# Packed attention and a three-way maximum layer: two of the three lists that order the work, written anew

## The chip, the cores and the metric

The kernel runs on one core of a Trainium2 chip. The metric is the device time of one execution in microseconds (us), as the median of several runs. TensorE is called PE below, VectorE DVE, ScalarE ACT, GpSimd POOL, and SyncE, which here does nothing but issue DMAs, SP.

## The reference

Eight batches, eight heads, 576 positions, 64 features per head, all in float32. First a few packed queries `p` look at keys and values, then the real queries look at what those have packed; the result goes through three matrices, of which the larger value counts, and a fourth.

```python
p_packed = sm_attn(p, k, v)                # softmax(p k^T / 8) v: 32 x 64 per head
out = sm_attn(q, p_packed, p_packed)       # 576 x 64 per head
x = out.transpose(0, 2, 1, 3).reshape(B * S, H * D)          # 4608 x 512
h = np.maximum(np.maximum(x @ w1, x @ w2), x @ w3)           # 4608 x 768
return (h @ w_out).astype(np.float32)                        # 4608 x 512
```

## The kernel before, in words

Everything is worked off batch by batch. For one batch: `scores` (PE, tile `s`) takes packed queries against keys; `weigh` is the exponential (a reduction on DVE, then ACT); `spread` turns the weights by two DVE transposes into `x` and by sixteen DMAs on SP (line 339) from `x` into `xt`; `values` (PE, tile `av`, line 357, 80 small matmuls) multiplies them with v; `packed` turns the result by one PE transpose (line 372), and it is copied into `pt`; `queries` (PE, tile `s2`, shown as `s` of line 386) takes q against `pt`; `attend` is the second softmax, a chain of some ten operations over DVE, POOL and ACT. Then `project` (tile `pw`) multiplies `pt` with the weights, `layer_in` (tiles `m...`) makes the products for the three-way maximum, `maximum` takes it on DVE (tile `r`), `halves` combines and splits `r` into high and low parts (`yah`, `yal`, `ybl`, `ych`, `ycl`, ...), `layer_out` (tiles `mo`) is the last product, and `finish` scales it and stores it (tiles `s`, `t`, `u`, `v` of line 813; the first two batches at line 736, with `r`). Each large float32 product is three matmuls on rounded parts (high by high, low by high, high by low), each 128 x 288.

Nothing but three lists of words sets the order. `START` does batches 0 and 1, converts the weights, and does the attention of batch 2; `LOOP` is run five times, for b = 2 to 6; `LAST` finishes batch 7. A word is a letter for a stage and the indices it is for; each time it stands in a list, the stage goes one step on. In `LOOP` the first digit is added to b, so that a run of it does the layers of batch b and the attention of batch b + 1: `S1` is `scores` of b + 1, `X1` `spread` (its third word issues the sixteen DMAs), `V101` `values`, `K1` `packed`, `Q1` `queries`, `N03` a step of `layer_in`, `H01` of `halves`, `B10` of `attend`. Lower-case words load: `v11` is v of batch b + 1 and its second half of the heads (two DMAs, lines 184 and 185), `q10`, `k20`, `w..` likewise. A letter at the end, `v`, `g` or `a`, puts a movable step onto DVE, POOL or ACT. `J2` has PE multiply the identity to no use (line 162).

Every engine, SP's queue too, works in the order of the list, and waits by semaphores. Of the tiles, k, v, q, `x`, `xt` and `r` share eight buffers, taken in the order of the list, and the products share four single PSUM banks and two double ones; an instruction that needs a buffer waits for the last reader of what lay there.

```python
nc.sync.dma_start(out=v[:, 0:SF, :], in_=va[u].rearrange("p (t x) -> p t x", x=256))
nc.sync.dma_start(out=v[0:SR, SF, :], in_=vb[u])
...
for c in range(4):
    n = len(range(c, NT, 4))
    for i in range(4):
        nc.sync.dma_start(out=at[NP * c:NP * c + NP, 0:n, i], in_=x[NP * i:NP * i + NP, c::4])
...
run(START, 0)
for b in range(2, B - 1):
    run(LOOP, b)
run(LAST, B - 1)
```

Of the kernel before, what the change touches and what calls it, by code (L numbers as in the profile page):

```python
# [52 lines left out]
C12 B011 B001 P00 C12 C12 J21 P01 k10 B000v B000 B010a B001 C20 w32 k11 w21 B000a B000g B010 B001a N00 B010v
B010 B010g C22 C22 P01 P00 B010g N00 B001 B011v B001g v11 J2 S1 v10 B011 P01 C32 C32 N01 N01 N01 C20 B011 w30
E000v C22 B011v B001 E010a A11 A11 A10 A10 E010 Z11 B001v C21 C20 C21 C22 N00 B001v B011 E000 A10 A11 q10 A10v
E000 q11 A11a N00 B011g B011 B011a V101 C20 C30 C30 w31 B011g Z10 E010 N01 V101 C21 C21 K1 C30 N00 w52 C31 K1v
C32 C32 Q1 N00 E011a E001a B10 C31 w41 P02 P02 B11 C52 P10 P10 B10 w40 B11 k20 C40 C41 C31 P02 N01 E011 C30
N01 C31 P03 B10g P03 E001 E001 C41 N02 N02 E020a N02 C52 N02 E011 k21 N02 H00g w42 B10 B11g P10 E021a P03 S2
C40 E020 C40 N03 N03 N03 v21 C41 C41 C42 E020 B11 C42 B10 E021 C52 E030a C42 A20 A20 A21 A21 w50 C50 w51 B11
B11a B10a X2 X2 C50 C50 C51 N02 C52 N03 C40 C42 P04 C51 C50 B10 E030 E030 P11 B11 N03 B11g N03 C51 B10g P04  # L60
C51 P04 E031a N04 N04 N04 P05 E031 B11 v20 B11a E040v E040 B10 H01a H01v N04 N04 N04 E021 w61 E031 H00a H00g
Z20 P05 w60 C60 P05 N05 E041a E041 N05 E041 C61 C61 B10g B10v H01v P11 B11g N10 E050a H02v E040 H04g N10 N10
C60 X2 Z21 H04a H02a V201 P11 N05 C60 H04v E100a C61 C61 E100 C60 E050 E050 w62 C62 N05 N05 E051a E051 N10 N10
w65 C65 E101a W0v W0g W0g R1v N11 w64 q20 V201 K2 K2a C65 C65 N11 N11 E110a E101 N11 w63 H03a H02v E110 E110
C65 H03v E100 W0a q21 C63 Q2 B20 B21 N11 N11 E111v E111 E111 W0g W0a C63 C63 P13 P15 C64 P13 P13 H03v C64 N10
C62 C62 N05 C64 P15 W0g P15 N13 N13 N13 H01v P12 W0g W0a C62 B21 P14 C63 E130a E051 P12 B21g N13 N13 N15 N15
E150a E101 E130 H01a P12 N12 W1g k30 C64 H10v N12 N12 W2g W2g E131v E131 E120a H03v W1g W1v E130 W2v E120 E120
W1a E150 N13 E131 H05a N12 N15 N15 W1v H05v H05g W2a W2v W2a H05g W0g E150 P14 P14 N12 N12 E121a E151a O0 N15
N14 N14 E121 E121 E151 B21 B21 B21v H01g B21 H03a B20 E140a N14 N14 N14 F0 W1a E140 E140 W2v W2v R2g O0 F0 W1v
O0 O0 E141a B21v H05a B20v B20 H03v H12v W1v F0 F0 H05v W2a H10a W1a W1g N14 E141 E141 N15 E151 H13g O0 F0 O0  # L70
O0 O0 O0 O0 O0 H11a H12a H12v H10v W2v k31 F0 R0v O0 O0 F0 F0 F0 H13v H14g H14a H13g H13v F0 O0 H11v H11g R3g
P22 P22 B20 B20v P20 B20 H11v F0 F0 F0 F0 H11a F0 F0 H14v B20v B21 H15a O1 O1 H13a H15v H15g H15v O1 O1 F1 P20
P20 O1 O1 H11v B20 H15a H15v H13v O1 P22 P22 P20 P20g P22g P22g F1 B21a F1 F1 F1 F1 F1 O1 O1 O1 F1 F1 R4g B20a
B20g T2g T2g P21 B21v T2v T2g T2a T2v O1 F1 F1 P20v P20g P21 P21 P21 P21 P21 P21 P21v P22v F1 F1 O1 O1 F1 P20a
P20v P20 T2a O1 P21g P21g P21a T2g R5g P22a P22g F1 P21g F1 P20 P20 P22
# [7 lines left out]
N02 E02 E02 P05 E02 E02 H01g H01g v11 N03 E03v P03a N02 E02 N03 N03 P03g E03a E03a N03 N03 H01g N03 N03 P05
E03 E03a P05v P05g E03 N03 P04 V101 P05v H02v E03 E03 E03 Z11 N03 P05g P04 P04 P04 P04 P04 P04 V101 V101 N04
P04g P04g K1 H02a N04 N04 K1a P04g P04a q10 H02v E04v E04a E03 Q1 P05g B10 B10 P04g N04 E04a H01a E04 N04 N04
N04 E04a E04 N04 N04 N05 E05a E04 H01g N05 N05 N05 E04 E05a E05a H03a A10 N05 N05 N05 E04 E04 B11 B10g B10
H04g H04g E05 P10 P12 B11 E05a P11 N05 H04v B11g P11 P12 P11 P11 P05 P12 E05 E05 N05 E05 B10 B10a O0 O0 O0 O0
E05 E05 F0 P11 B10 P11 P12 P11 P12v H05a H03g H03g H05v P10 H03v B11 F0 F0 H05g F0 B11 B11a B11 O0 O0 O0 H03a
P11g B10v B10 k21 F0 P10 F0 P11v P11g H03v O0 H05g H05a H05v O0 O0 P05 P12g P12g F0 F0 P05 F0 P10 P10g B10a
B10g B11g F0 B11 B11a P12a P10g O0 O0 T1g F0 O0 P10v P10g T1v F0 B11v T1v P11a T1v T1a T1v P10v T1a T1g P10  # L90
P11g F0 P10 O0 P10 F0 P12g P12 P12 P12
"""


# [810 lines left out]
```

## Time and profile before

| | |
|---|---|
| time, median of 3 runs | 463.65 us (462.92 to 464.65) |
| the profiled execution | 462.4 us, its span 460.3 us |
| granted clock of TensorE | 1.00 |
| PE busy | 451.2 us, 98% |
| DVE busy | 392.7 us, 85% |
| POOL busy | 290.3 us, 63% |
| ACT busy | 253.0 us, 55% |
| moved by DMA | 55.68 MB |

The span is from the first to the last instruction of the trace; the execution's own time is 2.1 us more, and the median 1.25 us above that. Matmuls overlap each other, so PE's busy share says that there is nearly always one in flight, not that none came late.

### The profile page before, as it was taken

To read this page: it belongs to the slowest core of one execution; us is meant where nothing else is said; L and a number is where in the kernel's file an instruction comes from. 1 tells how busy PE (TensorE), PEld (TensorE's weight loads), DVE (VectorE), ACT (ScalarE), POOL (GpSimd) and SP (SyncE) were. 2 spreads that over 40 slices of the span, in tenths; PEclk is the share of its full clock that TensorE was granted. 3 is DMA by queue.
4 is the path that set the end of the run, shared out by engine and by line. 5 is a ranking of instruction groups with operands and counts; after the bars stand their busy time and mean duration, and the time that the engine had idled before them with its cause. 6 is when DMAs were issued, how large, how long until landed. Compare 5 with 4: busy or idle time off the path is not lost.

```text
span 460.3 us, 11868 instructions
## 1 busy us (share of the span) xinstructions
PE 451.2 (98%) x4616; PEld 393.2 (85%) x4616; DVE 392.7 (85%) x820; ACT 253.0 (55%) x559; POOL 290.3 (63%) x296
## 2 busy tenths in 40 slices
...
GB/s 316 398 385 339 340 67 269 2 0 115 78 53 141 145 168 1 51 225 104 99 1 85 211 150 34 5 189 122 164 2 53 168 115 30 2 103 1 2 1 103
DMA packets 35783, 55.68 MB, mean 121 GB/s; under 512 B 17296, under 2 KB 26512, under 8 KB 35728
## 3 DMA queue, kind: packets, MB, share of 16 engines
...
q8 instruction: 36, 0.59, 0.5%
q14 instruction: 19, 0.16, 0.1%
...
## 4 chain that ended last, share of the span: by engine, by line
PE 87%; DMA 6%; DVE 5%; issue 1%; ACT 0%; SPq 0%; DVEq 0%
PE mo L784 22%; PE mi L630 12%; PE me L543 9%; PE mx L543 9%; PE pw L459 7%; PE mf L543 6%; PE mu L543 6%; PE mo L707 4%; PE my L543 3%; DMA q<-in_qt 3%; DMA wi<-in_wi 2%; PE av L357 2%; PE s L273 2%; PE s L386 2%; PE idle L162 1%; DMA v<-in_va 1%
## 5 line engine op out<-in xcount | busy, mean ns | idle before, releaser
L486 POOL TENSOR_TENSOR pf<-pf 128x128 f32<-128x128 f32 x73 | 40.8, 569 | 32.0 <-ACT pf L469 23.6
L672 POOL TENSOR_TENSOR r<-r 128x288 f32<-128x288 f32 (+1 forms) x46 | 49.3, 1079 | 14.5 <-DVE r L587 6.6
L477 DVE SCALAR_TENSOR_TENSOR pl<-pw,ph 128x384 fp32r<-128x384 f32 (+1 forms) x67 | 46.6, 719 | 4.1 <-ACT ph L475 3.8
L475 ACT ACTIVATE ph<-pw 128x384 fp32r<-128x384 f32 (+1 forms) x67 | 40.4, 638 | 7.7 <-PE pw L459 7.3
L630 PE MATMUL mi<-a2h,ph 128*128 128x288 f32 x144 | 44.3, 307 | 0.1
L469 ACT ACTIVATE pf<-pw 128x256 f32<-128x256 f32 (+1 forms) x54 | 22.2, 457 | 40.1 <-PE pw L459 40.1
L630 PE MATMUL mi<-a2l,ph 128*128 128x288 f32 x144 | 42.5, 295 | 0.0
L630 PE MATMUL mi<-a2h,pl 128*128 128x288 f32 x144 | 42.4, 295 | 0.0
L459 PE MATMUL pw<-w_sb,pt 64*32 64x384 f32 x768 | 38.3, 489 | 1.2 <-POOL w_sb L225 1.1
L153 POOL TENSOR_TENSOR sl<-pf,sh 128x384 fp32r<-128x384 f32 x30 | 30.5, 1026 | 12.1 <-ACT sh L148 11.8
L225 POOL TENSOR_TENSOR w_sb<-w_sb,wi 128x512 int32<-128x512 int32 x18 | 23.7, 1326 | 22.6 <-DVE w_sb L221 15.7
L630 PEld LDWEIGHTS mi<-a2h,ph 128*128 128x128 f32 x144 | 27.0, 188 | 7.0 <-issue 2.8
L543 PE MATMUL me<-a2h,ph 128*128 128x288 f32 x108 | 32.7, 303 | 0.0
L784 PE MATMUL mo<-ych,xl 128*128 128x288 f32 x108 | 31.9, 295 | 0.0
L543 PE MATMUL me<-a2l,ph 128*128 128x288 f32 x108 | 31.9, 295 | 0.0
L543 PE MATMUL me<-a2h,pl 128*128 128x288 f32 x108 | 31.9, 295 | 0.0
L784 PE MATMUL mo<-ych,xh 128*128 128x288 f32 x108 | 31.8, 295 | 0.0
L784 PE MATMUL mo<-ycl,xh 128*128 128x288 f32 x108 | 31.8, 294 | 0.0
L630 PEld LDWEIGHTS mi<-a2l,ph 128*128 128x128 f32 x144 | 27.0, 188 | 0.1
L630 PEld LDWEIGHTS mi<-a2h,pl 128*128 128x128 f32 x144 | 27.0, 188 | 0.0
L148 ACT COPY r<-me 128x288 f32<-128x288 f32 x25 | 10.0, 400 | 30.9 <-PE me L543 30.4
L543 PEld LDWEIGHTS me<-a2h,ph 128*128 128x128 f32 x108 | 20.3, 188 | 5.4 <-DVE r L587 3.1
...
## 6 DMA issues: line engine op xcount, KB each, us to landing
...
q<-in_qt SPq DMA_DIRECT2D x16, 576.0 KB, 5.0
...
```

The costliest lines, as they stand in the source:

```text
L153: on(default).tensor_tensor(out=lo, in0=src, in1=hi.bitcast(F32), op=ALU.subtract)
L225: nc.gpsimd.tensor_tensor(out=dst.bitcast(I32), in0=dst.bitcast(I32), in1=up, op=ALU.add)
L459: nc.tensor.matmul(out=ps[r][NP * n:NP * n + NP, 0:NW * P], lhsT=pt_sb[b % 2][o, NP * n:NP * n + NP], rhs=w_sb[o, j, n * NW * P:(n + 1) * ...
L469: nc.scalar.activation(out=f[:, r], in_=x[:, :, 0:2 * P], func=AF.Copy, scale=2.0 ** -WS)
L475: nc.scalar.activation(out=hi[:, r], in_=x, func=AF.Copy, scale=2.0 ** -WS)
L477: nc.vector.scalar_tensor_tensor(out=lo[:, r], in0=x, scalar=2.0 ** -WS, in1=hi[:, r].bitcast(F32), op0=ALU.mult, op1=ALU.subtract,)
L486: on("g").tensor_tensor(out=f[:, k], in0=f[:, x], in1=f[:, y], op=op)
L543: nc.tensor.matmul(out=ps[:, 0:HS], lhsT=w[wi], rhs=x[xi], start=first and n == 0, stop=n == 2, skip_group_check=not first,)
L630: nc.tensor.matmul(out=sums[b, j, hf, x][:, 0:HS], lhsT=w[:, r, x * P:(x + 1) * P], rhs=a[:, c], start=(r == 0 and n == 0), stop=(r == R - ...
L672: less = lambda out, x, y: on("g").tensor_tensor(out=out, in0=x, in1=y, op=ALU.subtract)
L707: nc.tensor.matmul(out=ps[:, 0:HS], lhsT=w[:, x, m * P:(m + 1) * P], rhs=h[:, z], start=(p == 0 and i == 0), stop=(p == NQ - 1 and i == 2),)
L784: nc.tensor.matmul(out=ps[:, 0:HS], lhsT=w[:, x, m * P:(m + 1) * P], rhs=h[:, z], start=(not onto and p == 0 and i == 0), stop=(p == NQ - ...
```

## The change

The text of `LOOP` is written anew, and that of `START` from the word `C12` of its fourth line on. `LAST` and all code are as before. The same steps are done; what differs is their order on each engine, and for some the engine. One dummy matmul, of the word `J2` ahead of batch 1's `scores`, is gone. The core of the diff is the head of `LOOP`:

```diff
-S1 A11 q11 k20 A10 N00 N00 N00 E00a v10 E00a E00v A10 N00 E00 N00 N00 X1 E00a E00 N00 E00 N00 N00 A11 P03 P05
-P03 P03 X1 E00 E00 N01 E00 P03 P03 P03 P03 P03g P03v H00g H00v N01 N01 N01 H00g E01a E01a E01v N01 E01 N01 X1
...
+v11 S1 N00 E00a N00 E00a A10 A10 N00 N00 A11 E00v N00 N00 E00 N00 E00a X1 A11 E00 N00 N00 E00 A11 P03 P03 P05
+N01 N01 N01 N01 X1 E00 E00 E00 P03 v10 P03 P03 q11 P03 k21 P03 E01a E01a N01 E01v E01 N01 N01 E01a N01 N01 E01
...
```

On SP's queue, one run of `LOOP` (b = 3) before. `v8` and `v9` are the two tiles of v of batch 4, `q8` and `q9` of q, `kt10` a tile of k of batch 5, and the sixteen DMAs of `xt4` stand as eight and eight:

```order
L193 DMA q9_2930<-in_qt 128x1152
L178 DMA kt10_2932<-in_kp 128x1280
L184 DMA v8_2955<-in_va 128x1024
L185 DMA v8_2955<-in_vb 64x256
L339 DMA xt4_3064<-x4_2974 32x5x64 x8
L339 DMA xt4_3064<-x4_2974 32x4x64 x8
L184 DMA v9_3157<-in_va 128x1024
L185 DMA v9_3157<-in_vb 64x256
L193 DMA q8_3318<-in_qt 128x1152
L178 DMA kt11_3597<-in_kp 128x1280
```

The same run now:

```order
L184 DMA v9_2906<-in_va 128x1024
L185 DMA v9_2906<-in_vb 64x256
L184 DMA v8_3035<-in_va 128x1024
L185 DMA v8_3035<-in_vb 64x256
L193 DMA q9_3042<-in_qt 128x1152
L178 DMA kt11_3045<-in_kp 128x1280
L339 DMA xt4_3198<-x4_2973 32x5x64 x8
L339 DMA xt4_3198<-x4_2973 32x4x64 x8
L193 DMA q8_3287<-in_qt 128x1152
L178 DMA kt10_3370<-in_kp 128x1280
```

Both tiles of v, one of q and one of k now stand ahead of the sixteen DMAs; before, the second tile of v stood behind them. The second tile of q is behind them in both.

On PE in the same run, from the transpose of `packed` to the first half of `s2` of batch 4, before; `me`, `mx` and `mu` are products of `layer_in` of batch 3:

```order
L372 MATMUL av4_3224<-ident_67,pp4_3291 128x128
L543 MATMUL mx3_4_3306<-a2h3_0_2826,ph3_4_3285 128x288
L543 MATMUL mx3_4_3306<-a2h3_0_2826,pl3_4_3286 128x288
L543 MATMUL mx3_4_3306<-a2l3_0_2828,ph3_4_3285 128x288
L543 MATMUL mu3_4_3310<-th3_0_2881,ph3_4_3285 128x288
L543 MATMUL mu3_4_3310<-th3_0_2881,pl3_4_3286 128x288
L543 MATMUL mu3_4_3310<-tl3_0_2883,ph3_4_3285 128x288
L386 MATMUL s2_4_0_3326<-q8_3318,pt0_73 32x288 x4
L386 MATMUL s2_4_0_3326<-q9_2930,pt0_73 32x288 x4
```

And now:

```order
L372 MATMUL av4_3229<-ident_67,pp4_3293 128x128
L543 MATMUL me3_4_3299<-a2h3_0_2828,ph3_4_3277 128x288
L543 MATMUL me3_4_3299<-a2h3_0_2828,pl3_4_3278 128x288
L543 MATMUL me3_4_3299<-a2l3_0_2830,ph3_4_3277 128x288
L543 MATMUL me3_4_3299<-a2h3_1_2841,ph3_4_3277 128x288
L543 MATMUL me3_4_3299<-a2h3_1_2841,pl3_4_3278 128x288
L543 MATMUL me3_4_3299<-a2l3_1_2843,ph3_4_3277 128x288
L386 MATMUL s2_4_0_3317<-q8_3287,pt0_73 32x288 x4
L386 MATMUL s2_4_0_3317<-q9_3042,pt0_73 32x288 x4
```

Before, twelve matmuls stood between `av` and the transpose and six between the transpose and `s2`; now it is six and six, so `s2` follows `av` six matmuls sooner.

On SP's queue in `START`, behind the sixteen DMAs for batch 2, before; `wi6_2` to `wi6_5` are pieces of the output weights, `q4` and `q5` are q of batch 2:

```order
L339 DMA xt2_1031<-x2_820 32x4x64 x8
L172 DMA wi6_2_1116<-in_wo 128x512
L172 DMA wi6_5_1149<-in_wo 128x512
L172 DMA wi6_4_1168<-in_wo 128x512
L193 DMA q4_1170<-in_qt 128x1152
L172 DMA wi6_3_1203<-in_wo 128x512
L193 DMA q5_1216<-in_qt 128x1152
```

And now:

```order
L339 DMA xt2_1001<-x2_831 32x4x64 x8
L172 DMA wi6_3_1166<-in_wo 128x512
L172 DMA wi6_2_1168<-in_wo 128x512
L193 DMA q5_1200<-in_qt 128x1152
L193 DMA q4_1206<-in_qt 128x1152
L172 DMA wi6_4_1333<-in_wo 128x512
```

Of the output weights' pieces, four stood between the sixteen and the second tile of q; now it is two, one (`wi6_5`) has gone ahead of the sixteen, and one follows q. On PE, 54 matmuls and the transpose stood between `av` of batch 2 and its `s2`; now it is 42 and the transpose.

Between the engines, one run of `LOOP` moves two steps from DVE to POOL, one `ycl` (128x864, line 153) and one product of `attend` (128x576, line 429), and two small ones of line 486; a split of 128x576 (line 153) and a subtraction of 128x288 (line 672) go from POOL to DVE, and the rounding copy `ych` (128x864) and the small `z` of line 425 from ACT to DVE. ACT takes one copy of 128x288 from DVE. In the changed part of `START`, DVE gives up fourteen instructions: one `ycl`, one split each of 128x576, 128x512, 128x384 and 128x288 (line 153), two combinations of 128x256 (line 237), a wide and a narrow subtraction (lines 672 and 415), one small `z`, and four copies out of PSUM. It gets seven: a copy of 128x256, a subtraction of 128x576 (line 415), two small ones of line 486, and one each of lines 505, 514 and 672. Most of what it gives up goes to POOL, whose instructions there rise from 88 to 93.

## Rows read from the trace of the kernel before

**Rows 1.** The page: busy us by engine; loads of q, median us to landing.

```profile
PE 451.2 (98%) x4616; PEld 393.2 (85%) x4616; DVE 392.7 (85%) x820; ACT 253.0 (55%) x559; POOL 290.3 (63%) x296
...
q<-in_qt SPq DMA_DIRECT2D x16, 576.0 KB, 5.0
```

**Rows 2.** Windows: length, busy us (instructions) by engine, granted clock, DMA share, GB/s.

```profile
90.00:127.00 37.00, 36.73 (x295) 35.21 (x294) 35.38 (x62) 17.79 (x34) 22.31 (x20) 1.00 0.20 64
...
233.00:286.00 53.00, 52.50 (x565) 47.09 (x563) 46.74 (x100) 29.45 (x69) 35.48 (x38) 1.00 0.34 104
```

**Rows 3.** Timeline of PE (start us, us): `av` of batches 2, 3, 5.

```profile
68.41 1.46 PE L357 MATMUL av<-v,xt 128*32 128x64 f32 x80
69.80 0.40 PE L630 MATMUL mi<-a2h,ph 128*128 128x288 f32 x1
...
165.02 1.94 PE L357 MATMUL av<-v,xt 128*32 128x64 f32 x80
166.88 0.40 PE L543 MATMUL mf<-a2h,ph 128*128 128x288 f32 x1
...
271.54 0.31 PE L357 MATMUL av<-v,xt 128*32 128x64 f32 x4
272.31 1.54 PE L357 MATMUL av<-v,xt 128*32 128x64 f32 x76 [0.47 <-DMA v<-in_va]
273.78 0.40 PE L543 MATMUL mf<-a2h,ph 128*128 128x288 f32 x1
```

**Rows 4.** Timeline of SP's queue (start us, us of issuing): batch 5 is fetched.

```profile
257.12 11.48 SPq L339 DMA_DIRECT2D xt<-x  x16
268.70 0.53 SPq L184 DMA_DIRECT2D v<-in_va  x1
270.37 0.33 SPq L193 DMA_DIRECT2D q<-in_qt  x1
```

**Rows 5.** DMA traffic of 250 to 275 us in 40 slices of 0.625 us.

```profile
GB/s 354 65 0 0 100 335 155 273 398 368 410 416 410 399 256 89 17 11 63 64 66 66 66 53 53 53 53 53 53 53 34 84 262 408 254 117 292 361 166 57
```

**Rows 6.** Timeline of PE: `s2` of batch 5; two products six matmuls apart.

```profile
276.47 1.20 PE L386 MATMUL s<-q,pt 64*32 64x288 f32 x32
...
278.50 0.29 PE L543 MATMUL me<-a2h,ph 128*128 128x288 f32 x1
279.30 0.31 PE L543 MATMUL mx<-th,sh 128*128 128x288 f32 x1
```

**Rows 7.** Timeline of SP's queue: the rest of batch 2's loads.

```profile
66.89 1.48 SPq L172 DMA_DIRECT2D wi<-in_wo  x3
...
70.98 1.20 SPq L193 DMA_DIRECT2D q<-in_qt  x1
```

**Rows 8.** Timeline of PE: `s2` of batch 2, from q's second tile on.

```profile
79.41 0.72 PE L386 MATMUL s<-q,pt 64*32 64x288 f32 x16 [0.99 <-DMA q<-in_qt]
```

**Rows 9.** Timeline of PE: two waits for DVE, then the dummy.

```profile
126.25 0.40 PE L707 MATMUL mo<-yal,xh 128*128 128x288 f32 x1 [0.27 <-DVE yal L153]
...
133.88 0.40 PE L707 MATMUL mo<-ycl,xh 128*128 128x288 f32 x1 [0.60 <-DVE ycl L153]
...
29.27 0.59 PE L162 MATMUL idle<-ident 128*128 128x256 f32 x2
29.80 0.47 PE L273 MATMUL s<-kt 64*32 64x288 f32 x8
```

**Rows 10.** Timelines of DVE and POOL around 122 us.

```profile
118.87 0.76 DVE L672 TENSOR_TENSOR r<-r 128x576 f32<-128x576 f32 x1
...
122.20 1.87 DVE L672 TENSOR_TENSOR r<-r 128x576 f32<-128x576 f32 x1
...
122.03 1.43 POOL L755 TENSOR_TENSOR t<-v,t 128x576 f32<-128x576 f32 x1
```

**Rows 11.** Groups by form: xcount | busy us, mean ns | idle before, releaser.

```profile
L153 DVE TENSOR_TENSOR ycl<-r,ych 128x864 fp32r<-128x864 f32 x18 | 20.2, 1153 | 0.8 <-POOL ych L150 0.8
...
L153 POOL TENSOR_TENSOR ycl<-r,ych 128x864 fp32r<-128x864 f32 x6 | 12.4, 2060 | 2.2 <-ACT ych L148 2.2
```

More of the change, by code (lines that the diff above doesn't have):

```diff
@@ L52 @@
 B000 B001 B000 B001v B000v C10 C10 C11 C11 C11 B000 C11 B000 B010 w20 C12 J11 P00 P00 w22 B011 P00 B000a B000
[L53 to L75, printed above, removed]
+C12 B011 B001 P00 C12 C12 J21 P01 k10 B000v B000 B010a B001 C20 w32 k11 w21 B000a B000g B010 B001a w30 v11
@@ new lines @@
+B010v C20 v10 B001 B010 B010g B010g B011g P00 N00 B001g P01 P01 C32 C32 B011 N00 C20 S1 C20 C22 B011 B001 A10
+B001g N00 B011v C22 q10 B011 B011g N01 N01 A11 E000a A10 A10 N01 B011 q11 C22 E010a E010 E010 A11 A11 E000
+E000 B001g A10a B011a C32 A11a N00 C21 C30 C30 Z11 w31 C22 C21 B011g Z10 V101 V101 N01 w52 K1 E011a C32 K1a
+N00 E001a C31 C31 Q1 C21 C21 C30 C30 B10 C52 w41 B11 w40 C31 C31 N00 E001 P02 B11 P02 P10 P10 P02 C41 C41 N01
+E011 N01 k20 B11g w42 E001 H00g C52 B10 B10g P03 P03 N02 B11 N02 N02 N02 E020a P10 P03 C42 C40 B10 C41 E021a
@@ new lines @@
+C52 C52 E020 E020 k21 C41 B11 E011 B11a B10 N02 C40 C40 N03 C42 C42 S2 N03 N03 N03 C40 A20 N02 C42 A21 E021
+E030a w51 C51 w50 A20 v21 X2 A21 w60 P04 C50 C50 X2 C50 P11 C51 C50 C51 P04 H00a B10a E030 E030 B11 P04 N03
+E031a E031 N03 C60 C60 B10 B11g B11 B11a E021 N04 E040a v20 B10v C51 E031 B10 N04 E040 P05 N04 N04 P05 B11v
+N04 N04 P05 w65 E041a E041 E041 w61 H00g N05 N05 N05 H03a H03g C61 X2 Z20 E040 B10a H01a N05 E051a B10v N10
+E050v E050 H02g H02a E050 H01v H01g C60 N10 N10 H04v C65 C65 C61 C61 H01v V201 E100a C61 C60 Z21 W0g V201 N10
@@ new lines @@
+N10 P11 P11 E100 N11 K2 H02v E101a N11 w63 w62 E100 K2v W0g N05 H03v C63 E110a E110 N11 W0g N11 q21 H03g W0a
+W0g R1v q20 Q2 W0a C65 C65 C62 E051 N11 H03a N11 E101 P13 C63 C63 B21 P15 B20 E111v E111 E111 E110 H04a W0g
+N05 P13 P13 E051 W0g H01a C63 P15 N10 P15 N13 N13 N13 H04v w64 C64 C64 E130a E130 C62 C62 C64 N13 E131v W0a
+E130 P12 H05a P14 C62 B21 N13 N13 P12 P12 H05g N15 E150a E131 E131 B21v N12 N12 P14 N12 W1g N15 W1g C64 E101
+H10v N12 E120a E120 E120 B21 W1g P14 E150 W2g W2v W1a N14 E140a W2v H05v H05g W0g W1v W1g N15 E150 N15 E151a
@@ new lines @@
+B21 B21a R3v W1g B21 N12 N14 E140 E121a E121 W2a W2v N12 W2a E121 N14 E140 N14 N14 N14 E141a E141 E141 B20 N15
+N15 O0 F0 O0 B20v W2v W2v H14v B20 R2v E151 E151 W1g H12g O0 O0 O0 F0 F0 H01v W2g W2v H05a H10a H03g H05v O0
+F0 H10v H13a F0 F0 H11a H11v H11g O0 H13v W1v F0 W1g O0 F0 R0g H12a H12v O0 F0 H13g O0 O0 O0 B21v B21 k30 H14g
+H11v H11a H15a O0 O0 F0 F0 P20 H13v F0 F0 B20 P22 P22 P22 H14v O1 O1 O1 B20v B20 F0 F0 H15v B20g H13a F0 H15v
+H15v H11v H13v F1 F1 F1 B20 H15a H15g O1 O1 O1 O1 O1 P20 O1 k31 P20 P20 P20v P22 B20a B20g F1 F1 B21a B21v F1
@@ L76 @@
+F1 P21 O1 O1 O1 P21 F1 P22g P21 T2g T2v T2g P20v P20g F1 T2v P22g T2a F1 T2v P21 P21 P21 P21 P21v P22v F1 P21g
+P21v T2a F1 T2g P20a P20g P20 P22a O1 O1 F1 F1 R5g F1 R4g P22g P21a F1 P20 P21g P22 P20
 """
 LOOP = """
-S1 A11 q11 k20 A10 N00 N00 N00 E00a v10 E00a E00v A10 N00 E00 N00 N00 X1 E00a E00 N00 E00 N00 N00 A11 P03 P05
-P03 P03 X1 E00 E00 N01 E00 P03 P03 P03 P03 P03g P03v H00g H00v N01 N01 N01 H00g E01a E01a E01v N01 E01 N01 X1
-E01a N01 N01 N01 E01 N02 N02 N02 E01 P05 E01 E01 E01 E02a E02a A11 Z10 P03g E02a N02 N02 N02 N02 H01g E02 E02a
@@ L83 @@
[L83 to L91, printed above, removed]
+v11 S1 N00 E00a N00 E00a A10 A10 N00 N00 A11 E00v N00 N00 E00 N00 E00a X1 A11 E00 N00 N00 E00 A11 P03 P03 P05
+N01 N01 N01 N01 X1 E00 E00 E00 P03 v10 P03 P03 q11 P03 k21 P03 E01a E01a N01 E01v E01 N01 N01 E01a N01 N01 E01
@@ new lines @@
+E01 H00g H00g N02 N02 H00g P03v P05 P05 P03g P03g P03a N02 N02 E01 E01 E01 E02v E02a Z10 N02 N02 E02a P05 P05g
+P05g H01v N02 E02 H01g E02a N02 E02 E02 E02 E02 N02 N03 N03 E02 E03a E03a P05v P03g Z11 H01v H02g P05g N03 N03
+N03 N03 E03a N03 E03 E03a E03 X1 N03 H01g P04 V101 H02a E03 E03 P04 P04 P04 N03 q10 P04 P04 H01a V101 P04 K1
+K1a N04 P04g P04g P04v H02v P04a P05g P04g Q1 N04 N04 A10 E04a E04a N04 N04 E04a N04 N04 E03 E03 B10 H01g B10
+B10g k20 E04 E04a N04 E04 E04 E04 N04 H03g H03g N05 N05 N05 N05 E04 E04 H04g B11 B11 E05a E05a N05 N05 E05a
```

5 lines of the change are left out of this document (added).

## Prediction

> **What bounds the kernel now.** I read the page first, then the windows, then PE's and SP's timelines at the places that the change touches. PE is busy for 451.2 of 460.3 us [rows 1], but its busy share counts overlapping matmuls, so what can be won there has to be read from the starts of successive rows. In a window one batch long PE is busy 52.50 of 53 us, DVE 46.74, POOL 35.48; at the end of the first batches DVE is almost as full as PE, 35.38 of 37 us [rows 2]. So PE sets the time; a gain can come only where PE waits, or from a matmul that is dropped; and DVE sets what PE waits for in the first batches. The clock is 1.00 in each window, and I take it to stay.
>
> The wait that returns with every run of `LOOP` is at `av`. The 80 small matmuls of `av` of batch 2 take 1.39 us from their first start to the next product (68.41 to 69.80). For batch 3 the same work takes 1.86 us, for batch 5 2.24, with an idle time of 0.47 put down to the DMA of v [rows 3]; batches 4, 6 and 7 repeat it with 1.86, 1.97 and 1.74. SP's timeline says why: the second tile of v is issued at 268.70, behind the sixteen DMAs, which hold the queue from 257.12 for 11.48 us [rows 4], and `av` goes on only at 272.31 [rows 3].
>
> **The change, part by part.**
>
> *The loads of v ahead of the sixteen.* The second tile of v is now issued before 257.12, more than ten microseconds ahead of its `av`. All five `av` of `LOOP` should take 1.39 us: 0.47, 0.47, 0.85, 0.58 and 0.35, together 2.7 us. The bounds are 0 (something else holds `av`, the sixteen themselves) and 2.7; I take 2.7, because the idle time in the row names v.
>
> *What that puts in front of the sixteen.* One more tile (512 and 64 KB) stands ahead of them. In the traffic of that stretch, the four loads that now stand ahead fill the slices up to about 259.4 us at 370 to 416 GB/s, and the sixteen go on alone at 53 to 66 [rows 5]. Another 0.58 MB at 400 GB/s is 1.45 us, so the loads would be through near 260.9, while the last of the sixteen is issued at 268.6 either way. Cost: 0, hidden in the sixteen's own issuing; if that cover were gone it is the slower rival below. The Trainium skill, "DMA: Bandwidth & Descriptors", Queues, rings and completion order, speaks against the change here: on each DMA engine descriptors are consumed in the order of the ring, so that the sixteen cannot pass the loads. By that rule the first of them land later and the last do not, and the sum stays; the traffic above agrees as far as it goes.
>
> *`s2` six matmuls sooner.* Six 128x288 matmuls are 0.80 us from start to start (278.50 to 279.30), 0.133 each. For batch 5 `s2` starts at 276.47 [rows 6]; without the wait of 0.85 and the six matmuls it would be wanted at 274.8. Its second tile of q is issued at 270.37, when `x`, whose buffer it takes, has been read [rows 4]; that order is unchanged. The traffic of this tile ends near 274.4 [rows 5], 4.0 us on, a margin of 0.4; the page's median of 5.0 [rows 1] would make it 275.4, a wait of 0.55. Between these ends I take 0 to 0.2 a batch, nearest to the row of this stretch, where moreover v's tile is no longer just ahead.
>
> *The other steps of a run.* By counts and mean durations DVE has some 0.6 us less to do in a run and POOL 2.0 more: the `ycl` that moves costs 1153 ns on DVE and 2060 on POOL [rows 11]. Both stay under PE's 53 us. Each engine's new order can make small waits of its own that no row shows; bounds 0 and 0.6 a batch, which is the wait at `av` come back; I take 0.1 a batch with q's together, 0.5 in all. `LOOP` then gives 2.7 less 0.5, **2.2 us**. `LAST` is unchanged and DVE is under its load there too: 0.
>
> *q of batch 2.* Here `s2` waits: PE goes on at 79.41 after 0.99 us idle for q [rows 8]. From 66.89 on SP issued four pieces of output weights and both tiles of q, the second at 70.98 [rows 7]: 2.1 and 1.2 MB through by 79.4, 12.5 us. Now two pieces stand ahead of q, 2.2 MB, at the same rate 8.4 us, near 75.3. The tiles of q take the buffers of v and so wait for the end of `av` (69.80 before), and `s2` is wanted 42 matmuls later, 42 x 0.133 = 5.6 us, near 75.4. At the page's 5.0 us q lands at 74.8 to 75.3. I take 0.8 of the 0.99 as won; bounds 0 and 1.1.
>
> *DVE in the first batches.* Two waits of PE name DVE, 0.27 at 126.25 and 0.60 at 133.88, the second for a `ycl` [rows 9]. By counts and mean durations, DVE has 5.0 us less in the changed part of `START` and POOL 4.5 more. I take 0.7 of these 0.87 us. The other end is no gain and new waits of the same size, since a moved step takes about twice as long on POOL [rows 11]; the good end is 1.5, were the small holes that remain in PE's starts to close as well.
>
> *The dummy.* Between its start at 29.27 and the scores at 29.80 lie 0.53 us [rows 9]. Bounds 0 (PE would wait for the scores' buffer anyway) and 0.5; I take 0.3.
>
> **Sum.** `START` 0.8 + 0.7 + 0.3 = 1.8, `LOOP` 2.2, together 4.0 us. From the profiled execution's 462.4 that is 458.4. That execution lay 1.25 us under the median of the runs, so I forecast **459.7 us** against 463.65.
>
> **Rivals.**
>
> *POOL holds DVE, and only part of the gain comes (about 461.6).* The trace has it: the same subtraction of line 672 takes 0.76 us at 118.87 and 1.87 at 122.20, where POOL's 1.43 us from 122.03 run to 123.46, and DVE ends 0.61 us behind them [rows 10]. So a DVE operation on two operands in SBUF does nothing while such a POOL operation runs, and work moved to POOL comes back as DVE time. If each added microsecond of POOL held DVE for as much as here, 1.1 of 1.43, the 4.5 us in `START` would take 3.5 of DVE's 5.0, and the 2.0 in a run 1.5, more than the 0.6 it saves. Then nothing is won at DVE's two waits and 0.3 is lost elsewhere; q and the dummy give 0.8, and `LOOP` 1.3 with each run losing some 0.2 more: 2.1 less, 461.6. Against it: most DVE operations read PSUM or one operand, and DVE has six microseconds of room in a run. The Trainium skill says the same in "SBUF — State Buffer", SBUF: two separate sides: DVE, with two inputs in SBUF against a POOL operation that reads it, and POOL share a port pair under an exclusive lock. The trace agrees, at 122.20.
>
> *Nothing that can be measured (about 463.3).* The wait at `av` is gone, but PE, that much earlier, waits at the next place, a PSUM bank that DVE frees in `layer_out` or the copy of `pt`, and gets to the next `scores` as late as before. For it speaks that DVE is busy 88% of the window; against it that `layer_out` lies twenty microseconds after `av`, and that `pt` is an ACT copy of a transpose with six matmuls of cover on either side, as stood ahead of `s2` before.
>
> *Slower: the sixteen slip behind the loads (467 and more).* q's second tile waits for `x` to be read, so when the sixteen slip by t, `s2` waits t less the margin of 0.4, in five batches. At t = 1.2 us that is 4.0 and the gain is gone; from 1.7 the change is slower by more than 0.5%; 2 us make 467.7. It takes a queue that lets the sixteen start only once the loads are through (257.12 to about 260.9). Against it: loads were in flight during the first 2.3 us of the sixteen in the run before, too, and their issuing shows no hold beyond its 0.7 us each.
>
> **How the numbers follow.** A measurement of this kernel can tell about 0.5% (2.3 us) from no change. My forecast case, 457.3 to 461.3, has 0.63, and a still larger gain 0.04. The POOL rival, 461 to 462.5, has 0.17, of which 0.03 end as faster. No measurable change has 0.08. The slower rival, with what else could go wrong in an order of over three thousand rows, has 0.08. So faster 0.70, same 0.22, slower 0.08. The range of 8 in 10 is 457.2 to 463.3: it leaves out the upper half of the no-change case, the slower case and the larger gain, some 0.16.
>
> **What would show it.** On SP's queue: both tiles of v issued before the sixteen, which still take 11 to 11.5 us. On PE: all five `av` at about 1.39 us, no idle time for v, and `s2` of `LOOP` without one for q; from the scores of one batch to those of the next some 0.45 us less than before, and the first scores of `LOOP` 1.8 us sooner. In the first batches: no wait of 0.99 for q, and the waits for `yal` and `ycl` below 0.2 us together. Wrong would be: `s2` that waits for q in each batch, idle time of PE for `pl` or a freed bank in `layer_out`, or rows of DVE around moved POOL steps that are a microsecond longer than their like.

## The result and the profile after

The changed kernel takes 460.48 us (median of 20 runs; all but one lie from 456.29 to 464.64), the kernel before 463.26 beside it (461.65 to 468.16). The ratio is 0.992 with an interval of 0.989 to 0.995, that is 3.75 us (2.5 to 5.0) less. It compares fast runs alone and so leaves out one run of 538.05 us at a granted clock of 0.75 and five from 463.8 to 464.6 of the changed kernel, and one of 468.16 of the kernel before; the medians of all runs give 2.8 us. The profiled execution took 460.18 us, its span is 458.4, the granted clock 1.0.

The forecast was 459.7, with the ratio almost as measured. The way there was another. The page, busy time by engine; it answers to [rows 1]:

```profile
PE 446.1 (97%) x4614; PEld 391.5 (85%) x4614; DVE 391.2 (85%) x808; ACT 254.8 (56%) x556; POOL 306.5 (67%) x311
```

PE is busy 5 us less in a span only 2 us shorter: it waits more than before. The table of waits says for what (engine, line, releaser: us in total, times, longest):

```profile
PE s L386 <- DMA q<-in_qt: 3.3, 3, 1.8
PE av L357 <- DMA xt<-x: 1.5, 1, 1.5
```

No wait for v is left. In its place stand waits for the two things that SP issues last: the sixteen DMAs of `xt`, and q's second tile. The timeline of PE (start us, us, then idle time before and its releaser): `av` of batches 3 and 4, `s2` of batch 5, and two rows of batch 2; they answer to [rows 3, 6, 8, 9]:

```profile
162.91 0.31 PE L357 MATMUL av<-v,xt 128*32 128x64 f32 x6
164.76 1.41 PE L357 MATMUL av<-v,xt 128*32 128x64 f32 x74 [1.54 <-DMA xt<-x]
166.10 0.40 PE L543 MATMUL mf<-a2h,ph 128*128 128x288 f32 x1
...
217.76 1.46 PE L357 MATMUL av<-v,xt 128*32 128x64 f32 x80
219.15 0.40 PE L543 MATMUL mf<-a2h,ph 128*128 128x288 f32 x1
...
275.36 1.21 PE L386 MATMUL s<-q,pt 64*32 64x288 f32 x32 [1.78 <-DMA q<-in_qt]
...
78.06 0.72 PE L386 MATMUL s<-q,pt 64*32 64x288 f32 x16 [0.98 <-DMA q<-in_qt]
81.53 0.88 PE L459 MATMUL pw<-w_sb,pt 64*32 64x384 f32 x16 [0.47 <-DVE e L409]
```

`av` takes the foreseen 1.39 us in batches 4, 6 and 7 (217.76 to 219.15), but 3.19 in batch 3 and some 1.6 in batch 5. `s2` starts 1.85 us late in batch 5, and 0.65 in batches 3 and 6. (In batch 6 the profile names a copy of ACT that ends in the same moment; but q landed at 328.15 and `s2` starts at 328.29, 0.14 later, as it does in batches 3 and 5.)

SP's queue as batch 5 is fetched, and the chain of waits of the same stretch (start us, us, what); they answer to [rows 4]:

```profile
253.85 0.38 SPq L178 DMA_DIRECT2D kt<-in_kp  x1
255.49 13.35 SPq L339 DMA_DIRECT2D xt<-x  x16
270.22 0.33 SPq L193 DMA_DIRECT2D q<-in_qt  x1
```

```profile
253.85 8.81 DMA kt<-in_kp
...
262.67 0.58 SPq L339
...
268.25 1.90 DMA xt<-x
...
270.22 5.00 DMA q<-in_qt
```

The sixteen take 13.35 us, where they took 11.48. The seventh starts at 259.66; the eighth is issued at 262.67, in the moment in which k, issued at 253.85, has landed (262.66). The other batches show the same: from the start of the seventh to that of the eighth it is 2.86, 2.25, 3.01 and 2.09 us in batches 3 to 6, where most starts lie 0.65 apart, and the eighth starts at 156.20, 209.86, 262.67 and 316.34, where k landed at 156.18, 209.84, 262.66 and 316.33. SP stands idle for 1.5 to 2.4 us of each gap. In batch 7, for which no k is loaded ahead, SP is never idle between them and the sixteen take 11.10 us. Below, this idle time of SP is called the hold. What comes behind a late sixteenth is late too: x is read until 270.15 (268.25 and 1.90), q's second tile is issued at 270.22 and lands at 275.22, 5.00 us later.

Why k and the eighth? Here are SP's DMAs in the order of the program, for one run of `LOOP`, with the semaphores for which each waits (`DMAHW` are those that landings raise): k, the first, the seventh and the eighth of the sixteen, and q's second tile.

```
L178 DMA kt_3045<-in_kp 128x1280 [waits DMAHW3_49,Pool_49]
L339 DMA xt_3198<-x_2973 32x5x64 [waits DMAHW4_49,DVE_49,PE_49]
...
L339 DMA xt_3198<-x_2973 32x5x64 [waits DMAHW2_49]
L339 DMA xt_3198<-x_2973 32x5x64 [waits DMAHW3_49]
...
L193 DMA q_3287<-in_qt 128x1152 [waits DMAHW4_49,DMAHW5_49,DMAHW3_49,DMAHW6_49,DMAHW2_49,DMAHW7_49,DMAHW1_49,DMAHW0_49]
```

The program gives SP's DMAs eight semaphores in turn, and a DMA waits until the one before it on its semaphore, the eighth ahead of it, has landed. The landing of k raises `DMAHW3`; with k last ahead of the sixteen, the eighth of the sixteen waits for it. The traces bear the rule out over all of SP's DMAs: in all thirteen, those of the experiments included, no DMA starts less than 16 ns after the landing of the eighth before it, while 16 to 36 in each start before the seventh has landed.

How long the parts of the program take is read from the first row of `scores` of three batches; the first ones, then batch 3 and batch 7 in the changed kernel:

```profile
5.20 0.69 PE L273 MATMUL s<-kt 64*32 64x288 f32 x8
...
141.86 1.20 PE L273 MATMUL s<-kt 64*32 64x288 f32 x32
...
356.57 1.20 PE L273 MATMUL s<-kt 64*32 64x288 f32 x32
```

Before, these rows start at 5.93, 144.34 and 357.77. So up to batch 3, mostly the work of `START`, it takes 136.66 us instead of 138.41, 1.75 less; but the four batches of `LOOP` from there take 214.71 instead of 213.43, **1.28 more**. About 0.4 of that is `START`'s: PE waits 0.44 us for DVE at 149.52, and 0.34 to 0.46 at that place in all ten traces with the new `START`, in none of the three with the old. The rest of the gain in this execution lies in the first loads (0.73) and behind the scores of batch 7 (0.70), where the fifth `av` of `LOOP` stands. These are readings of one execution. The changed kernel's runs lie 8 us apart, where the quickest versions below keep within 1 us.

### The profile page after: what moved, and what is told of

Same layout as the page of the kernel before. It is cut to its first block, busy times and chain, and to the rows that moved or that the text cites. A ratio compares the mean times of both kernels' runs of the same rounds, so it can differ in the third digit from the quotient of the medians.

```text
span 458.4 us, 11890 instructions
## 1 busy us (share of the span) xinstructions
PE 446.1 (97%) x4614; PEld 391.5 (85%) x4614; DVE 391.2 (85%) x808; ACT 254.8 (56%) x556; POOL 306.5 (67%) x311
## 4 chain that ended last, share of the span: by engine, by line
PE 72%; DMA 12%; DVE 6%; POOL 3%; SPq 2%; ACT 2%; issue 2%; DVEq 0%; ACTq 0%; POOLq 0%
PE mo L784 18%; PE mi L630 11%; PE mx L543 8%; PE me L543 7%; PE pw L459 6%; PE mu L543 5%; PE mf L543 5%; DMA kt<-in_kp 4%; DMA wi<-in_wi 4%; PE mo L707 3%; DMA q<-in_qt 3%; PE my L543 3%; SPq L339 2%; PE s L386 2%; PE s L273 2%
## 5 line engine op out<-in xcount | busy, mean ns | idle before, releaser
L672 POOL TENSOR_TENSOR r<-r 128x288 f32<-128x288 f32 (+1 forms) x41 | 44.4, 1084 | 30.1 <-DVE r L587 15.4
L486 POOL TENSOR_TENSOR pf<-pf 128x128 f32<-128x128 f32 x81 | 41.6, 532 | 17.9 <-ACT pf L469 12.5
L475 ACT ACTIVATE ph<-pw 128x384 fp32r<-128x384 f32 (+1 forms) x67 | 41.2, 641 | 11.8 <-PE pw L459 6.1
L153 POOL TENSOR_TENSOR sl<-pf,sh 128x384 fp32r<-128x384 f32 x31 | 32.3, 1048 | 9.9 <-ACT sh L148 9.8
L153 POOL TENSOR_TENSOR ycl<-r,ych 128x864 fp32r<-128x864 f32 x12 | 29.9, 2488 | 3.2 <-ACT ych L148 3.2
L148 ACT COPY r<-me 128x288 f32<-128x288 f32 x30 | 12.0, 398 | 35.3 <-PE me L543 34.8
```

Of the source, the lines that this page charges most:

```text
L153: on(default).tensor_tensor(out=lo, in0=src, in1=hi.bitcast(F32), op=ALU.subtract)
L475: nc.scalar.activation(out=hi[:, r], in_=x, func=AF.Copy, scale=2.0 ** -WS)
L486: on("g").tensor_tensor(out=f[:, k], in0=f[:, x], in1=f[:, y], op=op)
L672: less = lambda out, x, y: on("g").tensor_tensor(out=out, in0=x, in1=y, op=ALU.subtract)
```

## The experiments

Each was timed beside the kernel before, on one of three chips (there it took 462.74, 462.16 or 462.45 us); gains are by the ratio to it. "LOOP" below is the time of the four batches from the scores of batch 3 to those of batch 7: 213.43 before, 214.71 after. It is read from one profiled execution of each version.

**The new `START` with the old `LOOP`.** Only the text of `START` is that of the change.

> Only START is the new one; LOOP is that of before. Theory H (the loads that now stand ahead of the sixteen DMAs hold SP inside them, x is read later, q's second tile lands later and PE waits at s2): the gain of START stands alone, from the first scores to those of batch 3 136.7 us as in the changed kernel (138.4 before); the sixteen of LOOP take 11 to 11.5 us, s2 does not wait, av waits 0.35 to 0.85 us as before; periods 53.2 to 53.7; time 1.5 to 2.5 us under before, with the small spread of before. Rival L (LOOP's new order brings the gain, START's next to nothing): no measurable change.

Measured: 461.64 us (460.8 to 463.69), ratio 0.997 (0.996 to 0.999), 1.2 us less. `START` is as short as in the changed kernel (136.07), but LOOP takes 215.02, 1.6 more than before, which I had not expected; the sixteen are at 10.7 to 11.4 us, and `av` waits for v in each batch, from 1.59 to 2.51 us in all instead of 1.39. Of batch 5:

```profile
271.31 1.54 PE L357 MATMUL av<-v,xt 128*32 128x64 f32 x76 [0.74 <-DMA v<-in_va]
```

**The old `START` with the new `LOOP`.** The other half.

> Only LOOP is the new one. Theory H: the sixteen take 12 to 13.7 us in batches 3 to 6, s2 waits for q in some of them by 0.6 to 1.9 us, av for xt in one or two; the five periods together are as long as before within 1.5 us, and the time is within 1.5 us of before, with a spread of several us from run to run. Rival L: 2.2 us less than before or better, with a small spread.

Measured: 461.83 us (457.33 to 465.72), ratio 0.994 (0.991 to 0.997), 2.8 us (1.3 to 4.2) less. The sixteen take 13.43, 12.93, 12.26 and 14.29 us in batches 3 to 6 and 10.76 in batch 7, LOOP 215.44, and the spread of 8 us comes with this half. `av` of batch 3, `s2` of batch 6, and a window (length, then busy us (instructions) of PE, its loads, DVE, ACT and POOL, clock, DMA share, GB/s):

```profile
165.84 1.41 PE L357 MATMUL av<-v,xt 128*32 128x64 f32 x74 [1.88 <-DMA xt<-x]
...
330.23 1.21 PE L386 MATMUL s<-q,pt 64*32 64x288 f32 x32 [0.93 <-DMA q<-in_qt]
...
167.40:170.80 3.40, 3.40 (x21) 2.92 (x28) 2.55 (x7) 0.99 (x3) 0.99 (x2) 0.50 0.84 299
```

Part of the length and of the spread is TensorE's clock. It is granted at 0.50, that is 1.2 GHz, from 167.40 to 170.80, shortly after PE stood idle for 1.88 us at `av`; from the product behind `av` to the one behind `s2` it takes 4.52 us here, and 3.04 where k stands behind the sixteen (below). The twelve runs go by their mean granted clock: 457.3 to 460.3 us at 0.999 to 1.0, 461.7 to 463.8 at 0.996, 464.7 to 465.7 at 0.992 to 0.993. That the wait made the clock fall is likely but no run changes it alone.

By the ratios the halves gain 1.2 and 2.8 us, together about what the change gains; the second is more than the 1.5 that theory H allowed, though its interval reaches down to 1.3. Neither comes near what the next run shows.

**k behind the sixteen.** In the changed kernel k's tile moves from ahead of the sixteen to the other tile of k; the loads of v stay in front.

```diff
-... P03 v10 P03 P03 q11 P03 k21 P03 E01a ...
+... P03 v10 P03 P03 q11 P03 P03 E01a ...
...
-... B10g k20 E04 ...
+... B10g k21 k20 E04 ...
```

> The changed kernel with one load moved in LOOP: k21 stands behind the sixteen, beside k20, so that 1.73 MB instead of 2.37 stand ahead of them. Theory H: the sixteen take 11 to 11.5 us, q's second tile lands some 2 us sooner, no wait at s2 and none at av; the four periods from batch 3 to 7 fall from 214.7 to about 210, the time to about 456, and the spread from run to run shrinks to some 2 us. Rival R (the hold costs nothing by itself; what PE waits for is set by the order of DVE and POOL): the sixteen get shorter but the waits stay or move to another product, 459 to 461.

Measured: 454.39 us (453.78 to 454.53), ratio 0.981 (0.977 to 0.984), 8.9 us less than before: 5.2 more than the whole change, for one word moved. SP's queue and PE's timeline for batch 5:

```profile
252.91 11.39 SPq L339 DMA_DIRECT2D xt<-x  x16
264.40 0.53 SPq L193 DMA_DIRECT2D q<-in_qt  x1
268.87 0.88 SPq L178 DMA_DIRECT2D kt<-in_kp  x2
```

```profile
267.39 1.46 PE L357 MATMUL av<-v,xt 128*32 128x64 f32 x80
268.77 0.40 PE L543 MATMUL mf<-a2h,ph 128*128 128x288 f32 x1
...
270.68 1.20 PE L386 MATMUL s<-q,pt 64*32 64x288 f32 x32
```

No hold, all `av` at 1.39, no wait at `s2`: this is the picture that the prediction drew. LOOP takes 209.37 (141.80 to 351.17). But q is issued at 264.40, before x can have been read: with k gone from there, q's second tile gets the buffer that was k's. So two things changed at once, and the next runs part them.

**q ahead, k behind.** `k21` and `q10` change places in the changed kernel: both tiles of q stand ahead of the sixteen, k behind.

> The changed kernel with two words of LOOP exchanged: q10 stands ahead of the sixteen, where k21 stood, and k21 behind them, where q10 stood. Bytes ahead 2.31 MB, nearly as now, but k instead of q takes the buffer of x. Theory H: the sixteen are still held by 1 to 2 us in each of batches 3 to 6, av waits for xt by 0 to 1.8 us, but s2 waits no more, since q does not need x's buffer; time about 457. Rival R: s2's wait was only named q and goes on for the copy of pt or a PSUM bank, 459 to 461.

Measured: 455.49 us (455.38 to 457.52), ratio 0.985 (0.982 to 0.988). The hold stays, on q instead of k (sixteen 12.82 to 14.10 us), and `av` comes late for `xt` in three batches (by 0.94 at most), yet `s2` never waits, since nothing stands behind the sixteen that it needs; LOOP 210.43. Of batch 6:

```profile
304.49 14.10 SPq L339 DMA_DIRECT2D xt<-x  x16
...
319.95 1.44 PE L357 MATMUL av<-v,xt 128*32 128x64 f32 x74 [0.33 <-DMA xt<-x]
```

So most of the hold's price was paid at q's second tile.

**k's buffer taken early, its DMA issued late.** The word `h21` at k's old place only takes the tile; `k21` beside `k20` issues the DMA. It was meant to keep q in x's buffer.

> The changed kernel with the buffers dealt out exactly as in it (k21's tile is taken where k21 stood, q's second tile takes x's buffer), but k21's DMA issued behind the sixteen. It parts the two things that the run with k behind changed together. Theory H (the 0.64 MB of k ahead hold SP inside the sixteen): the sixteen take 11 to 11.5 us, q's second tile is issued when x has been read, some 2 us sooner than in the changed kernel, s2 waits 0 to 0.2, time 454 to 455.5. Rival B (the hold matters little, q was late because it waits for x's buffer, and the run with k behind won by giving q another): q still waits at s2 by 0.3 us or more per batch, 456.5 to 459.

Measured: 454.13 us (453.8 to 454.8), ratio 0.983 (0.982 to 0.985), sixteen 11.1 to 11.8 us. It did not separate anything: the early word did not change how the buffers were dealt. q's second tile had the same buffer as with k behind, not x's, and was issued at 159.43, before x's last reader landed at 160.65.

**k behind, q's second tile put into x.** This keeps the buffer by force: from batch 3 on, q's second tile is loaded into x's own tile.

```diff
...
+    if b >= 3 and g == 0:
+        loaded["q", b, g] = x_of[b].rearrange(...)
...
```

> The kernel with k behind the sixteen, with q's second tile of batches 3 to 7 loaded into x's own tile, so that it must wait until the sixteen have landed, as in the changed kernel. This parts hold and buffer, which the two runs with k behind did not (there SP issued q before x had been read). Theory H: q is issued some 1.2 us later than with its own buffer and lands 22 to 23 us after the scores, s2 is wanted after 24: no wait, 454 to 455. Rival B (q's buffer was what cost time): s2 waits 0.3 us or more in each batch, 456 and more.

Measured: 455.39 us (454.94 to 455.41), ratio 0.984 (0.983 to 0.986). The sixteen are free of the hold but for 0.7 us in batch 3, where the eighth waits for q's first tile; q's second tile waits for x, and `s2` comes late once, by 0.42 us in batch 3; LOOP 210.49. Of batch 4:

```profile
201.00 11.62 SPq L341 DMA_DIRECT2D xt<-x  x16
214.08 0.33 SPq L195 DMA_DIRECT2D x<-in_qt  x1
```

So LOOP takes 209.37 us with neither hold nor x's buffer for q, 210.49 with x's buffer for q, 210.43 with a hold (q ahead, k behind), and 214.71 with both, the change: about 1.1 us for either alone and 5.3 for the two together. Some 3 us are paid only where a late sixteenth holds back q. The two small prices are rough, one execution each: of the 1.1 in this run 0.4 is at `s2` of batch 3 and the rest at other products in batches 4 to 6, for which no run shows q as the cause.

**More DMAs ahead, the same bytes.** On k behind, v's loads are cut into three DMAs instead of two and one of q into two: eight DMAs and 1.73 MB ahead of the sixteen, without k.

> The kernel with k behind the sixteen, with the loads ahead of them cut into more DMAs (eight in place of five for the same 1.73 MB; from batch 3 on each tile of v in three in place of two, one tile of q in two). If bytes in flight hold the sixteen: as without the cut, 11 to 11.7 us, time 454 to 455.5. If the number of DMAs or of their descriptors in the queue holds them: 12.5 us and more in batches 3 to 7, and av waits for xt; 456 or more.

Measured: 454.54 us (453.89 to 454.9), ratio 0.984 (0.982 to 0.986). The sixteen take 11.24 to 12.35 us, less than the 12.5 of the second theory. A clear hold comes once, in batch 7, where the seventh starts 2.56 us after the sixth, at 363.93, and q's first half, the eighth before it, landed at 363.91. PE waits for neither `xt` nor q in LOOP. So more DMAs for the same bytes can make a hold too, and here it costs nothing.

**k issued by POOL.** In the changed kernel k's DMA ahead of the sixteen goes to POOL's queue; it no longer counts among SP's eight.

```diff
-    nc.sync.dma_start(out=kt, in_=kp[u])
+    (nc.gpsimd if b >= 4 and g == 1 else nc.sync).dma_start(out=kt, in_=kp[u])
```

> The changed kernel with one load of k of each batch from 4 on, the one that stands ahead of the sixteen, issued by POOL in place of SP, so that as many bytes are in flight but SP's own list is one DMA shorter. Theory E (SP issues no DMA before the eighth of its own before it has landed, so that the load of k, the last ahead, stops the eighth of the sixteen): no long hold, the sixteen take 11 to 12 us in batches 3 to 6, s2 waits less, 454 to 457. Rival (the bytes in flight hold them, whoever issued them): 12 to 14 us, waits at s2 as in the changed kernel, 458 to 462.

Measured: 458.27 us (457.93 to 459.44), ratio 0.991 (0.990 to 0.993). My figures for the sixteen were wrong: 13.31, 12.79, 13.73 and 14.11 us. Now, in batches 4 to 6, the last of SP's own loads, q, holds the queue, and it takes 8.8 to 9.9 us to land, beside k, where it takes 6.1 to 7.0 with k behind. In batch 3 the tenth of the sixteen waits for the second, which lands at 156.50, 8.2 us after its start. The chain, and k's landing (KB each, median us from issue to landing):

```profile
251.08 9.85 DMA q<-in_qt
...
260.95 0.59 SPq L339
```

```profile
kt<-in_kp POOLq DMA_DIRECT2D x4, 640.0 KB, 9.7
```

So the eight semaphores decide which landing the sixteen wait for, and the bytes in flight when it comes. Taking k off the queue does not help; taking it out of that stretch does.

**Only the second tile of v moved.** The kernel before with one word moved.

```diff
-... E00a v10 E00a ...
+... E00a v11 v10 E00a ...
...
-... H01g H01g v11 N03 ...
+... H01g H01g N03 ...
```

> The kernel before, with one word moved in LOOP: v11 stands beside v10 ahead of the sixteen, so that 2.37 MB stand there as in the change, all else as before. Theory H: the sixteen take 12 to 14 us in batches 3 to 6 and about 11 in 7 (no k there), av waits for v no more but in some batches for xt, s2 waits for q in some; no gain, 462 to 465, with a spread of several us. Rival (the loads' order was a pure gain and the rest of the new LOOP made the waits): 2.5 us less than before, sixteen at 11.

Measured: 457.1 us (455.84 to 458.51), ratio 0.990 (0.988 to 0.992): 4.9 us less, where the whole change gives 3.75. My expectation of 462 to 465 was wrong. The sixteen are held here as well, now for v (12.4 to 12.5 us in batches 3 to 6; a gap ends at 261.44, v landed at 261.43), but SP is idle for only 0.8 to 1.2 us of each gap; here k and q had been issued some microseconds earlier. `s2` comes late by 0.36 and 0.44, and LOOP takes 210.91. Of batch 5:

```profile
255.74 12.39 SPq L339 DMA_DIRECT2D xt<-x  x16
```

```profile
270.21 1.46 PE L357 MATMUL av<-v,xt 128*32 128x64 f32 x80
...
274.71 1.20 PE L386 MATMUL s<-q,pt 64*32 64x288 f32 x32 [0.37 <-DMA q<-in_qt]
```

**The new `START`, and two words of `LOOP`.** The old `LOOP` with `v11` moved as above and `k20` moved behind the sixteen, to `k21`.

> START is the new one, LOOP that of before with two words moved: v11 beside v10 ahead of the sixteen, k20 beside k21 at the end of the run. Everything else that the new LOOP changes is missing. Theory D (of the new LOOP only the places of the loads count; its other moves between and on the engines are worth nothing): the sixteen take 11 to 11.5 us, av 1.39, no wait at s2, periods 52.3, time within 1 us of the run with k behind, 454 to 455.4. Rival (the other moves in LOOP give something too): 456 or more.

Measured: 454.55 us (454.2 to 455.01), ratio 0.983 (0.981 to 0.984). LOOP takes 209.80 (141.12 to 350.92), with the new text of `LOOP` and k behind 209.37. The rest of the rewriting of `LOOP` is worth nothing that can be measured. The sixteen take 11.1 to 12.3 us; SP is held for v by 1.0 and 1.3 us in batches 4 and 6, and PE does not wait for it: `av` takes 1.39 us in all batches, and `s2` is never late.

**k behind, and q of batch 2 before the weights.** `START` with `q21 q20` ahead of `w63 w62`, against the wait of 0.98 us for q.

> The kernel with k behind the sixteen, and in START q of batch 2 ahead of the two pieces of output weights (q21 q20 w63 w62 in place of w63 w62 ... q21 ... q20). s2 of batch 2, which waits 0.8 to 1.3 us for q, would not wait: 0.7 us less, about 453.7. Against it: the pieces of weights then wait behind q for the end of av, 4 us later, and their conversion can hold DVE or POOL, then PE, and take it back: 454.4 or more.

Measured: 457.7 us (457.0 to 458.04), ratio 0.991 (0.989 to 0.992), 4.4 us less than before, where k behind alone gave 8.9. ACT is idle for 5.88 us until the first piece of the weights lands at 77.27, and converts it before it copies what PE waits for:

```profile
78.28 0.40 PE L630 MATMUL mi<-a2h,ph 128*128 128x288 f32 x1 [3.64 <-ACT r L148]
```

Here, too, the clock is granted at 0.5 behind the long wait, for 3.4 us from 79.1 on. That is the smaller part: the four runs at a mean clock of 0.996 take 457.7 to 458.0 us, the two at 1.0 457.0 and 457.4.

## Why the prediction came out right

The time was right by two errors that met: `LOOP` had more to win than I counted, and the hold, which I did not count, took it back. Nearly without the hold, and with q's second tile in x's buffer as in the change, the time is 455.4 us, 7 under the kernel before on the same chip, where the forecast was 4.0. That the two errors came to the same size is luck.

**The wait at `av`: right, and under-sized in its effect.** Nothing waits for v any more, and in the three batches without a late `xt`, `av` is at 1.39 us. With no hold or a short one, LOOP takes 210.49 us with q in x's buffer, 2.9 less than before, and 209.4 to 209.8 where q has another, 3.6 to 4.1 less. In these four batches `av` had 2.4 to give (0.47, 0.47, 0.85, 0.58), and the forecast, less 0.1 a batch, was 2.0. Set row against row, the version with two words gains on the kernel before at the product that follows `av`, as foreseen, and by another 0.5 us in each of the four batches at two products, `mu` and `my`, some 8 us later, which no term foresaw. DVE, POOL and PE in the kernel before (batch 4), then DVE and POOL with two words:

```profile
226.54 1.27 DVE L587 TENSOR_TENSOR r<-u,r 128x288 f32<-128x288 f32 x1
227.73 0.44 DVE L587 TENSOR_TENSOR r<-mx,r 128x288 f32<-128x288 f32 x1
...
226.32 1.17 POOL L415 TENSOR_TENSOR e<-e,m 128x576 f32<-128x576 f32 x1
...
228.23 0.40 PE L543 MATMUL mu<-th,ph 128*128 128x288 f32 x1
```

```profile
222.28 0.57 DVE L587 TENSOR_TENSOR r<-u,r 128x288 f32<-128x288 f32 x1
...
222.49 1.38 POOL L415 TENSOR_TENSOR e<-e,m 128x576 f32<-128x576 f32 x1
```

In the program `mu` waits until DVE has read `mx`, and that stands behind DVE's `r<-u,r`. Before, POOL's subtraction begins 0.22 us ahead of this operation, which then takes 1.27 us, and `mu` starts at 228.23, 0.06 after `mx` has been read. With two words DVE begins first and takes 0.57, and POOL takes 1.38 instead of 1.17. In all five batches of LOOP POOL is first in the kernel before, and DVE with two words; with only the second tile of v moved, of batches 3 to 6 it is DVE in 4 and 6, and there alone the 0.5 us come. It is what the POOL rival told of, here as a gain. The 0.5 us for new waits was hardly needed.

**What that puts in front of the sixteen, "Cost: 0, hidden in the sixteen's own issuing": this step failed.** I read the traffic (the loads through near 261, the last of the sixteen issued at 268.6 either way) and took the queue to go on issuing meanwhile. It does not: SP holds a DMA until the eighth before it has landed, and with k last of 2.37 MB ahead of the sixteen (two tiles of v, one of q, one of k), SP stands idle for 1.5 to 2.4 us in the middle of them. The slower rival named the effect (the sixteen slip by t, and q and `s2` with them) and its price. Its t is here the time by which the sixteen grew: 3.0, 1.2, 1.9, 1.7 and 0.2 us in batches 3 to 7. By its rule, t less 0.4 in each batch, that costs 6.2 us; measured are 3.1 at `s2` and 2.0 at `av`. What I had against the rival, an issuing that shows no hold in [rows 4], was true of the kernel before, where fewer bytes were in flight ahead. The rule of the Trainium skill that I weighed there ("DMA: Bandwidth & Descriptors", Queues, rings and completion order) is about descriptors already in a ring. By it, as I worked it out, the last of the sixteen would land no later; the runs show it landing later, since it is issued later.

**`s2` with a margin of 0.4 us: the order right, the margin read too large.** q's issue follows x's last reading, as said. But q's tile of batch 5 lands 4.44 us after its issue in the trace before, not the 4.0 that I read from the traffic, so that hardly any margin was there. And the term "0 to 0.2 a batch" supposed sixteen that are not late: it came out where k is behind and q in x's buffer (0.42 once in five batches). Measured in the change: 0.65, 0, 1.85, 0.64 and 0.

**`START`, 1.8 us: right in sum.** From the first scores to those of batch 3 it is 1.75 us less in the two profiled executions; over the nine executions that have this text and the three with the old one, 2.0 (135.9 against 137.9 on average). The parts are another matter. The wait for q of batch 2, which was to give 0.8, gave nothing that shows. It is 0.98 us here, as long as before, and in the nine executions with this text anything from 0 to 1.0, since q's second tile lands 4.8 to 6.8 us after its issue, where I took 5.0; but the next wait, for DVE at 81.53 (0.47 here), is longer by what this one is shorter: the two make 1.44 to 1.54 us in each of the nine, and from the scores of batch 1 to those of batch 3 it is always 112.8 us (113.5 to 114.9 with the old text). So q is no longer what PE's progress hangs on there. The waits for `yal` and `ycl` are gone, as foreseen. The dummy's part does not show: up to the scores of batch 1 it is 23.89 us, 23.87 before. What made the rest of the 1.8 no row names.

**DVE's relief, 5.0 us in `START`: the rival on POOL was right about the mechanism.** Windows from the scores of batch 1 to those of batch 3, and from there to batch 7, before and after (length, then busy us (instructions) of PE, its loads, DVE, ACT and POOL, clock, DMA share, GB/s):

```profile
29.80:144.30 114.50, 112.32 (x1181) 98.74 (x1180) 105.27 (x209) 67.16 (x131) 77.90 (x65) 1.00 0.41 142
144.30:357.80 213.50, 212.52 (x2266) 189.55 (x2267) 189.21 (x401) 118.18 (x277) 143.97 (x155) 1.00 0.34 106
```

```profile
29.10:141.90 112.80, 111.03 (x1187) 98.59 (x1189) 104.31 (x205) 70.15 (x136) 84.17 (x70) 1.00 0.43 147
141.90:356.60 214.70, 209.79 (x2266) 188.58 (x2266) 188.97 (x396) 117.82 (x272) 152.84 (x164) 1.00 0.35 105
```

POOL gained 6.3 and 8.9 us; DVE was relieved of 1.0 and 0.2. Over the whole execution DVE is busy 1.5 us less, where counts by mean durations said about 8. The same step has become longer on both, as `ycl` shows, which answers to [rows 11] (by form: xcount | busy us, mean ns):

```profile
L153 DVE TENSOR_TENSOR ycl<-r,ych 128x864 fp32r<-128x864 f32 x12 | 16.1, 1354 | 0.8 <-POOL ych L150 0.8
L153 POOL TENSOR_TENSOR ycl<-r,ych 128x864 fp32r<-128x864 f32 x12 | 29.9, 2488 | 3.2 <-ACT ych L148 3.2
```

1153 ns became 1354 on DVE and 2060 became 2488 on POOL. In the kernel before, DVE operations on two operands in SBUF that began during a POOL operation ended 0.61 to 0.62 us after that one's end for 128x576 (24 of 25) and 0.91 to 0.92 for 128x864 (5 of 5). The Trainium skill, "SBUF — State Buffer", SBUF: two separate sides, states an exclusive lock between the two for such operations. The trace agrees, with these figures; here moved work came back as longer work. PE lost little by it: its two waits for DVE went all the same, though DVE was hardly relieved, so that this term came true for another reason than mine; which, no run shows. The rival's price, not its mechanism, was wrong.

**What stays open.** What made `START`'s 1.8 us, and why the old `LOOP` behind the new `START` is slower (215.02) than behind the old one (213.43). Of these 1.6 us, 0.5 is the wait for DVE at its first products, and 0.7 lies at `av` (0.74 idle for 0.47 in batch 5), as though v landed later, but no run changes that alone.
